# Cosine-weighted linear attention with an MoE tail: cos and sin parts stacked along the contraction

## The chip, the cores and the metric

One core of a Trainium2 chip. The metric is the device time of one execution in microseconds (us), median of several runs. The engines in the profile: PE is TensorE (matmul), PEld its weight loads, DVE VectorE, ACT ScalarE, POOL GpSimd, SP the engine that issues most loads.

## The reference

```python
q, k, v: [8, 8, 576, 64] float32          # batch, heads, positions, head size
cos_w, sin_w = cos(pi/2 * pos/576), sin(...)           # one pair per position
phi(x) = concatenate([relu(x) * cos_w, relu(x) * sin_w], axis=-1)      # 64 -> 128
kv  = einsum('bhsf,bhsd->bhfd', phi(k), v);   z = sum over s of phi(k)
num = einsum('bhsf,bhfd->bhsd', phi(q), kv);  den = phi(q) . z + 1e-6
x   = (num / den) as [4608, 512]
h   = x @ w_in [512, 2048];  g = h * sigmoid(beta * h);  out = g @ w_out [2048, 512]
```

Dividing num by den cancels any factor of a query row. So the kernels use 1 and tan for the query's two halves in place of cos and sin.

## The kernel before

The tokens go through the MoE in nine chunks of 512. Each chunk has 32 slots on TensorE: 16 h groups (x @ w_in, then Silu on ScalarE), then 16 quarters of the out product. The attention of batch c+1 is slipped between the slots of chunk c. Batch 0 runs alone in a prologue, batch 1 beside chunk 0. A batch has 8 heads in 4 pairs of rows (j), 9 blocks (n) of 64 positions, and two halves (g) of the partitions. Line numbers in the profile mean: L260 the kv matmuls, L281 num, L366 h, L391 out.

```python
# keys: relu only; values: scaled twice, by cos and by sin; column D of vb holds cos or sin
vb = [P, NQ, 4, 2, E]; rk = [P, NQ, 4, D]; qb = [P, 2, NQ, 2*D]; qt, qs = [P, 2, NQ, P]
...
def kv_mm(b, jp, bank, jjs=(0, 1)):                       # 36 matmuls of 64x64, 130 columns (72 a batch)
    for n in range(NQ):
        for jj in jjs:
            for g in range(2):
                matmul(t[jj*HP:(jj+1)*HP, g], lhsT=rk[hs, n, 2*jp+jj, :],
                       rhs=vb[hs, n, 2*jp+jj] as (s e), start=(n == 0), stop=(n == NQ-1))
def num_mm(n, jp, bank, slot):                            # 8 matmuls of 64x64, 65 columns
    for cs in range(2):
        for jj in range(2):
            for g in range(2):
                matmul(ps[cols, bank+jj, ...], lhsT=(qt, qs)[cs][rows, jp, n, cols],
                       rhs=kv[rows, g, jp, cs, :], start=(cs == 0), stop=(cs == 1))
...
# prologue: GpSimd's part is two products with the broadcast table
take("act", 0); take("dve", 1)
v_scale(0, 1, 0, 0, 6, eng="pool")        # one tensor_tensor, 6 x 2 x 64 = 768 elements
take("act", 1)
v_scale(0, 1, 0, 6, NQ, eng="act")
v_scale(0, 0, 0); k_relu(0, 0, 2, "act", 0, 5); k_relu(0, 0, 2, "dve", 5, NQ); take("dve", 0)
kv_mm(0, 0, 6)
v_scale(0, 1, 1, 0, 5, eng="pool")        # one tensor_tensor, 640 elements
...
# q's tan part is made after the transpose: GpSimd multiplies qt by a tan table into qs
```

## Time and profile before

| | before |
|---|---|
| time | 296.71 us, median of 3 runs (296.6 to 297.01) |
| span in the profile | 295.0 us |
| TensorE busy | 286.8 us (97%) |
| GpSimd busy | 73.8 us, of which 29.3 us are q's tan products |
| first h group starts | 18.06 us |
| a steady chunk | 30.3 us |

The prediction below shows the lines that its argument rests on. Each line has the start, the length, the engine, the line, the operation, its output and inputs, and how many instructions were merged.

```profile
9.06 1.47 POOL L205 TENSOR_TENSOR vb<-raw_v,sin 128x768 bf16<-128x768 f32 x1 [6.90 <-ACT qt L235]
...
12.20 1.26 POOL L205 TENSOR_TENSOR vb<-raw_v,sin 128x640 bf16<-128x640 f32 x1 [1.67 <-DMA raw_v<-in_v_dram]
...
18.06 0.59 PE L366 MATMUL ps<-xt,win 128*128 128x512 bf16 x2
```

GpSimd needs two instructions for its share of batch 0, 2.7 us in all. The prologue is over when the first h group starts at 18.06.

### The profile page before, as it was taken

To read this page: it belongs to the slowest core of one execution; us is meant where nothing else is said; L and a number is where in the kernel's file an instruction comes from. 1 tells how busy PE (TensorE), PEld (TensorE's weight loads), DVE (VectorE), ACT (ScalarE), POOL (GpSimd) and SP (SyncE) were. 2 spreads that over 40 slices of the span, in tenths; PEclk is the share of its full clock that TensorE was granted. 3 is DMA by queue.
4 is the path that set the end of the run, shared out by engine and by line. 5 is a ranking of instruction groups with operands and counts; after the bars stand their busy time and mean duration, and the time that the engine had idled before them with its cause. 6 is when DMAs were issued, how large, how long until landed. Compare 5 with 4: busy or idle time off the path is not lost.

```text
span 295.0 us, 7173 instructions
## 1 busy us (share of the span) xinstructions
PE 286.8 (97%) x3058; PEld 142.8 (48%) x3058; DVE 116.3 (39%) x296; ACT 140.1 (47%) x223; POOL 73.8 (25%) x88
## 2 busy tenths in 40 slices
PE   8799999999999999999999999999999999999994
PEld 7454455455445544454445544554455444444443
DVE  5989978662920293019500960077005000000000
ACT  5758826563247214731474137512760277137510
POOL 1350003252382026402550256015701210000000
PEclk9999999999999999999999999999999999999999
DMA  7999999597999089916992599139102810130033
GB/s 259 366 393 379 387 389 393 197 288 268 163 259 361 4 125 219 383 62 120 217 379 76 113 231 397 45 67 196 44 2 46 146 37 0 41 84 19 0 73 71
DMA packets 50256, 53.82 MB, mean 182 GB/s; under 512 B 30880, under 2 KB 31152, under 8 KB 50224
## 3 DMA queue, kind: packets, MB, share of 16 engines
q1 hardware_dynamic: 47504, 46.01, 51.6%
q0 software_dynamic: 2688, 7.34, 10.7%
q8 instruction: 24, 0.39, 0.6%
q14 instruction: 8, 0.07, 0.1%
q10 hardware_dynamic: 32, 0.01, 0.0%
HBM read 36.71 MB, written 9.44 MB: 156 GB/s over the span
## 4 chain that ended last, share of the span: by engine, by line
PE 85%; DVE 5%; DMA 5%; ACT 2%; issue 1%; DVEq 0%
PE ps L366 38%; PE ps L391 38%; DMA w_stage<-in_moe_w_out_dram 5%; DVE win L108 4%; PE ps L281 4%; PE ps L260 3%; PE ps L407 1%; PE ps L416 1%; ACT vb L213 1%; DVE qs L218 1%; DVE xs L303 0%; ACT g_t L373 0%; ACT rk L188 0%; PE ps L425 0%; PE ps L230 0%
## 5 line engine op out<-in xcount | busy, mean ns | idle before, releaser
L366 PE MATMUL ps<-xt,win 128*128 128x512 bf16 x576 | 128.1, 379 | 0.8 <-ACT g_t L373 0.5
L391 PE MATMUL ps<-wout,g_t 128*128 128x512 bf16 x560 | 124.5, 379 | 0.2 <-ACT wout L115 0.2
L373 ACT ACTIVATE g_t<-ps,beta 128x512 bf16<-128x512 f32 x144 | 98.4, 687 | 36.6 <-PE ps L366 36.6
L366 PEld LDWEIGHTS <-win 128*128 128x128 bf16 x576 | 55.3, 98 | 67.6 <-DVE win L108 1.4
L391 PEld LDWEIGHTS <-g_t 128*128 128x128 bf16 x560 | 53.9, 98 | 64.0 <-issue 0.4
L386 POOL DMA_DIRECT2D out_dram<-o_sb x56 | 36.5, 656 | 142.2 <-ACT o_sb L397 142.2
L397 ACT COPY o_sb<-ps 128x512 f32<-128x512 f32 x35 | 20.5, 586 | 98.2 <-PE ps L391 98.2
L218 POOL TENSOR_TENSOR qs<-qt,tanr 128x1152 bf16<-128x1152 bf16 x12 | 29.3, 2456 | 10.2 <-DMA qt<-qb 10.2
L272 DVE CAST kv<-ps 128x520 bf16<-128x520 f32 x6 | 4.2, 700 | 67.8 <-PE ps L260 67.8
L410 DVE COPY o_sb<-ps 128x256 f32<-128x256 f32 x1 | 0.4, 425 | 63.0 <-PE ps L407 63.0
L303 DVE TENSOR_TENSOR xs<-ps,rden 128x768 bf16<-128x768 f32 (+5 forms) x26 | 23.1, 890 | 0.8
L292 DVE TENSOR_TENSOR den<-ps,eps 128x12 f32<-128x12 f32 (+4 forms) x26 | 4.2, 161 | 33.5 <-PE ps L281 33.5
L215 DVE TENSOR_SCALAR vb<-raw_v,cos 128x256 bf16<-128x256 f32 x63 | 17.1, 347 | 0.0
L215 DVE TENSOR_SCALAR vb<-raw_v,sin 128x256 bf16<-128x256 f32 x54 | 14.7, 349 | 0.0
L281 PEld LDWEIGHTS <-qt 64*64 64x64 bf16 x576 | 10.6, 106 | 5.0 <-issue 4.3
L281 PE MATMUL ps<-kv,qt 64*64 64x65 bf16 x576 | 11.8, 195 | 0.4 <-ACT kv L270 0.2
L190 DVE TENSOR_SCALAR qb<-raw_q 128x1152 bf16<-128x1152 f32 x16 | 11.4, 752 | 1.3 <-DMA raw_q<-in_q_dram 1.3
L108 DVE CAST win<-w_stage 64x512 bf16<-64x512 f32 (+1 forms) x28 | 11.6, 414 | 0.6
L260 PE MATMUL ps<-vb,rk 64*64 64x130 bf16 x576 | 10.1, 218 | 1.6 <-ACT rk L188 1.6
L281 PE MATMUL ps<-kv,qs 64*64 64x65 bf16 x576 | 11.6, 193 | 0.0
L260 PEld LDWEIGHTS <-rk 64*64 64x64 bf16 x576 | 8.5, 106 | 5.7 <-issue 3.0
L281 PEld LDWEIGHTS <-qs 64*64 64x64 bf16 x576 | 10.4, 105 | 0.0
(56 smaller groups left out, 99.9 us busy)
## 6 DMA issues: line engine op xcount, KB each, us to landing
raw_v<-in_v_dram SPq DMA_DIRECT2D x7, 1152.0 KB, 10.2
raw_k<-in_k_dram SPq DMA_DIRECT2D x7, 1152.0 KB, 12.9
raw_q<-in_q_dram SPq DMA_DIRECT2D x7, 1152.0 KB, 7.4
out_dram<-o_sb POOLq DMA_DIRECT2D x56, 128.0 KB, 4.1
w_stage<-in_moe_w_out_dram SPq DMA_DIRECT2D x4, 1024.0 KB, 9.0
w_stage<-in_moe_w_in_dram SPq DMA_DIRECT2D x3, 1024.0 KB, 12.8
out_dram<-o_sb SPq DMA_DIRECT2D x14, 128.0 KB, 2.3
raw_q<-in_q_dram SPq DMA_DIRECT2D x2, 576.0 KB, 4.4
```

What stands on the lines that cost most here:

```text
L108: nc.vector.tensor_copy(o, a)
L190: nc.vector.tensor_scalar(dst, src, scalar1=0.0, scalar2=None, op0=ALU.max)
L215: nc.vector.tensor_scalar(o, a, scalar1=t[:, n : n + 1], scalar2=None, op0=ALU.mult)
L218: eng.tensor_tensor(dst.rearrange("q n (g p) -> q n g p", g=2), src.rearrange("q n (g p) -> q n g p", g=2), tanr[:, n0:n1].unsqueeze(2).to ...
L260: nc.tensor.matmul(t[jj * HP : (jj + 1) * HP, g], lhsT=rk[hs, n, 2 * jp + jj, :], rhs=vb[hs, n, 2 * jp + jj].rearrange("q s e -> q (s e)") ...
L281: nc.tensor.matmul(ps[cols, bank + jj, slot * E : (slot + 1) * E], lhsT=(qt, qs)[cs][rows, jp, n, cols], rhs=kv[rows, g, jp, cs, :], start ...
L303: nc.vector.tensor_tensor(o.rearrange("q j n s d -> q j (n s) d"), nv[:, :, a:z, :, 0:D].rearrange("q j n s d -> q j (n s) d"), rden[:, :, ...
L366: nc.tensor.matmul(ps[:, h_bank(c, jt)], lhsT=win[jt // 4][:, mi, (jt % 4) * P : (jt % 4 + 1) * P], rhs=xt[:, :, jp, g * HP : (g + 1) * HP ...
L373: nc.scalar.activation(g_t, ps[:, h_bank(c, jt)], AF.Silu, scale=beta[:, jt : jt + 1])
L386: eng.dma_start(out=out_v[bb, n][:, m0:m1], in_=o_sb[hf * HP : (hf + 1) * HP, m0:m1])
L391: nc.tensor.matmul(o_ps, lhsT=gs[c, jt][:, tt * P : (tt + 1) * P], rhs=wout[jt // 4][:, jt % 4, :], start=(jt == 0), stop=(jt == JT - 1))
L397: nc.scalar.copy(o_sb, o_ps)
```

## The change

The intent: stack the cos and the sin part of a head along the contraction. Keys are scaled (relu times cos, relu times sin) into one [positions, 128] operand, values are only cast, with a column of ones, and q gets its tan copy before the transpose. Then num needs no accumulation over cos and sin: one matmul with K=128 does both.

```diff
-    vb = one.tile([P, NQ, 4, 2, E], ...)     -    rk = one.tile([P, NQ, 4, D], ...)
+    vb = one.tile([P, NQ, 4, E], ...)        +    kb = one.tile([P, NQ, 4, 2, D], ...)
-    qt, qs [P, 2, NQ, P]                     +    qt [P, 2, NQ, 2, P]
...
+    def relu_scale(dst, src, kind, eng, n0, n1):
+        if eng == "dve":                      # fused, table broadcast from PSUM
+            for j in ...: nc.vector.scalar_tensor_tensor(dst[:, n0:n1, j], src, 0.0, t, op0=max, op1=mult)
+            return
+        for n in range(n0, n1):               # one instruction per block n
+            if eng == "act": nc.scalar.activation(dst[:, n], src[:, n], Relu, scale=t[:, n:n+1])
+            else: (nc.gpsimd if eng == "pool" else nc.vector).tensor_scalar(
+                      dst[:, n], src[:, n], scalar1=0.0, scalar2=t[:, n:n+1], op0=max, op1=mult)
...
     kv_mm:  lhsT=kb[hs, n, j] as (c d)  (64x128), rhs=vb[hs, n, j]  (65 columns)
     num_mm: 4 matmuls, lhsT=qt[:, jp, n, jj, cols]  (128x64), rhs=kv[:, g, 2*jp+jj, :]
...
 prologue:
-    v_scale(0, 1, 0, 0, 6, eng="pool")  ...  v_scale(0, 1, 1, 0, 5, eng="pool")
+    k_scale(0, 1, 0, "pool")            ...  k_scale(0, 1, 1, "pool", 0, 5)     # 9 and 5 pieces
 chunk 0:
+        1: lambda: q_turn_last(2, "dve"),     # transposes of block n=8, evicted on VectorE
-        25, 26: 18 transposes of batch 1      +   25, 26, 27: 36 transposes
 chunks 1 to 6:
-    (7, q_tan(b, 0)), (8, q_tan(b, 1)) on GpSimd
+    q_tan_all() on VectorE ahead of the DMA transpose of q, which doubles
```

(The order in which k and v are loaded is also swapped.)

More of the change, by code (lines that the diff above doesn't have):

```diff
@@ L120 @@
     GJ = [(0, 0), (0, 1), (1, 0), (1, 1)]
-    for name in "qvk":
+    for name in "qkv":
         for b in range(2):
@@ L128 @@
     nc.scalar.dma_start(out=beta16, in_=moe_beta.rearrange("(j p) -> j p", p=P))
+    load_raw(0, "k", 0, 2)
     load_raw(0, "v", 0, 2)
-    load_raw(0, "k", 0, 2)
-    load_raw(0, "v", 2, 4)
-    load_raw(0, "k", 2, 3)
-    load_raw(0, "k", 3, 4)
+    load_raw(0, "k", 2, 4)
+    load_raw(0, "v", 2, 3)
+    load_raw(0, "v", 3, 4)
     load_w("in", 0, 2)
@@ L151 @@
     eps9 = const.tile([P, NQ], FP32, name="eps9")
-    tanr = const.tile([P, NQ, HP], FP32, name="tanr")
     nc.scalar.activation(cos9, it9, AF.Sin, bias=halfpi, scale=-ANG)
@@ L161 @@
     make_identity(nc, ident)
-    vb = one.tile([P, NQ, 4, 2, E], BF16, name="vb")
-    rk = one.tile([P, NQ, 4, D], BF16, name="rk")
-    qb = one.tile([P, 2, NQ, 2 * D], BF16, name="qb")
-    qt = one.tile([P, 2, NQ, P], BF16, name="qt")
-    qs = one.tile([P, 2, NQ, P], BF16, name="qs")
-    kv = one.tile([P, 2, 2, 2, E], BF16, name="kv")
+    vb = one.tile([P, NQ, 4, E], BF16, name="vb")
+    kb = one.tile([P, NQ, 4, 2, D], BF16, name="kb")
+    qb = one.tile([P, 2, NQ, 2, 2, D], BF16, name="qb")
+    qt = one.tile([P, 2, NQ, 2, P], BF16, name="qt")
+    kv = one.tile([P, 2, 4, E], BF16, name="kv")
     xs = one.tile([P, NQ, 2, 2 * D], BF16, name="xs")
@@ L174 @@
     nc.vector.tensor_scalar(eps9, eps9, scalar1=EPS, scalar2=None, op0=ALU.mult)
-    for cs, t in ((0, cos9), (1, sin9)):
-        nc.vector.tensor_copy(vb[:, :, :, cs, D], t.unsqueeze(2).to_broadcast([P, NQ, 4]))
+    nc.vector.memset(vb[:, :, :, D], 1.0)
     xts = {}
@@ L190, in relu @@
             nc.vector.tensor_scalar(dst, src, scalar1=0.0, scalar2=None, op0=ALU.max)
-    def q_relu(b, jp, eng="dve"):
-        relu(qb[:, jp].rearrange("q n (j d) -> q j n d", j=2), raw_tile(b, "q")[:, 2 * jp : 2 * jp + 2], eng)
-    def k_relu(b, j0=0, j1=4, eng="dve", n0=0, n1=NQ):
-        relu(rk.rearrange("q n j d -> q j n d")[:, j0:j1, n0:n1], raw_tile(b, "k")[:, j0:j1, n0:n1], eng)
-    def v_scale(b, cs, jp=None, n0=0, n1=NQ, eng="dve"):
-        t = (cos9, sin9)[cs]
-        rv = raw_tile(b, "v")
-        js = slice(0, 4) if jp is None else slice(2 * jp, 2 * jp + 2)
-        if jp is not None and eng != "act":
-            if eng == "dve":
-                t = ps[:, 0, 16 * cs : 16 * cs + NQ]
-            (nc.gpsimd if eng == "pool" else nc.vector).tensor_tensor(
-                vb[:, n0:n1, js, cs, 0:D],
-                rv.rearrange("q j n d -> q n j d")[:, n0:n1, js],
-                t[:, n0:n1].unsqueeze(2).unsqueeze(3).to_broadcast([P, n1 - n0, 2, D]), op=ALU.mult)
+    SC = {"cos": (cos9, 0), "sin": (sin9, 16), "tan": (tan9, 32)}
@@ L209, in v_scale @@
+    def relu_scale(dst, src, kind, eng, n0, n1):
+        t, col = SC[kind]
+        if eng == "dve":
+            t = ps[:, 0, col : col + NQ]
+            for j in range(dst.shape[2]):
+                nc.vector.scalar_tensor_tensor(
+                    dst[:, n0:n1, j], src[:, n0:n1, j], 0.0,
+                    t[:, n0:n1].unsqueeze(2).to_broadcast([P, n1 - n0, D]), op0=ALU.max, op1=ALU.mult)
             return
         for n in range(n0, n1):
-            o, a = vb[:, n, js, cs, 0:D], rv[:, js, n, :]
@@ L212, in v_scale @@
             if eng == "act":
-                nc.scalar.activation(o, a, AF.Copy, scale=t[:, n : n + 1])
+                nc.scalar.activation(dst[:, n], src[:, n], AF.Relu, scale=t[:, n : n + 1])
             else:
-                nc.vector.tensor_scalar(o, a, scalar1=t[:, n : n + 1], scalar2=None, op0=ALU.mult)
-    def tan_mul(eng, dst, src, n0, n1):
-        eng.tensor_tensor(
-            dst.rearrange("q n (g p) -> q n g p", g=2), src.rearrange("q n (g p) -> q n g p", g=2),
-            tanr[:, n0:n1].unsqueeze(2).to_broadcast([P, n1 - n0, 2, HP]), op=ALU.mult)
@@ L222, in q_turn_pe @@
-    def q_turn_pe(b, jp, bank, hold=False):
-        parts = ((0, 0, 5), (1, 5, NQ))
-        v2 = []
-        for i, n0, n1 in parts:
-            t = ps[:, bank + i].bitcast(BF16)[:, 0 : (n1 - n0) * P].rearrange("q (n c) -> q n c", c=P)
-            v2.append(t)
-            for n in range(n0, n1):
-                nc.tensor.matmul(t[:, n - n0, :], lhsT=qb[:, jp, n, :], rhs=ident,
-                                 is_transpose=True, start=(n == n0), stop=(n == n1 - 1))
-        def take(e, i):
-            _, n0, n1 = parts[i]
-            if e == "act":
-                nc.scalar.copy(qt[:, jp, n0:n1], v2[i])
-            else:
-                tan_mul(nc.vector, qs[:, jp, n0:n1], v2[i], n0, n1)
-        if hold:
-            return take
-        for e, i in (("act", 0), ("dve", 1), ("act", 1), ("dve", 0)):
-            take(e, i)
@@ L244, in q_turn_dma @@
-    def q_turn_dma(b):
-        nc.sync.dma_start(out=qt.rearrange("q s n c -> q (s n) c"),
-                          in_=qb.rearrange("q s n c -> q (s n c)"), transpose=True)
-    def q_tan(b, jp):
-        tan_mul(nc.gpsimd, qs[:, jp], qt[:, jp], 0, NQ)
-    def kv_out(jp, bank):
-        return ps[:, bank : bank + 2, jp * 2 * E : (jp + 1) * 2 * E]
-    def kv_mm(b, jp, bank, jjs=(0, 1)):
-        t = kv_out(jp, bank)
-        for n in range(NQ):
-            for jj in jjs:
+                (nc.gpsimd if eng == "pool" else nc.vector).tensor_scalar(
+                    dst[:, n], src[:, n], scalar1=0.0, scalar2=t[:, n : n + 1], op0=ALU.max, op1=ALU.mult)
@@ new lines, in q_relu, with q_tan, q_tan_all @@
+    def q_relu(b, jp, eng="dve"):
+        relu(qb[:, jp, :, :, 0].rearrange("q n j d -> q j n d"), raw_tile(b, "q")[:, 2 * jp : 2 * jp + 2], eng)
+    def q_tan(b, jp, eng, n0=0, n1=NQ):
+        relu_scale(qb[:, jp, :, :, 1], raw_tile(b, "q")[:, 2 * jp : 2 * jp + 2].rearrange("q j n d -> q n j d"),
+                   "tan", eng, n0, n1)
+    def q_tan_all():
+        for n in range(NQ):
+            nc.vector.tensor_scalar(qb[:, :, n, :, 1], qb[:, :, n, :, 0], scalar1=tan9[:, n : n + 1],
+                                    scalar2=None, op0=ALU.mult)
@@ new lines, in k_scale, with v_cast, q_turn_pe @@
+    def k_scale(b, cs, jp=None, eng="each", n0=0, n1=NQ):
+        js = slice(0, 4) if jp is None else slice(2 * jp, 2 * jp + 2)
+        relu_scale(kb[:, :, js, cs], raw_tile(b, "k")[:, js].rearrange("q j n d -> q n j d"),
+                   ("cos", "sin")[cs], eng, n0, n1)
+    def v_cast(b, j0=0, j1=4, eng="dve"):
+        o, a = vb[:, :, j0:j1, 0:D].rearrange("q n j d -> q j n d"), raw_tile(b, "v")[:, j0:j1]
+        (nc.scalar.copy if eng == "act" else nc.vector.tensor_copy)(o, a)
+    def q_turn_pe(blocks, bank):
+        for i, (jp, n, jj) in enumerate(blocks):
+            nc.tensor.matmul(ps[:, bank + i // 8].bitcast(BF16)[:, (i % 8) * P : (i % 8 + 1) * P],
+                             lhsT=qb[:, jp, n, jj].rearrange("q c d -> q (c d)"), rhs=ident,
+                             is_transpose=True, start=(i % 8 == 0), stop=(i % 8 == 7 or i == len(blocks) - 1))
@@ new lines, in q_turn_half, with q_take, q_turn_last @@
+    def q_turn_half(jp):
+        return [(jp, n, jj) for n in range(8) for jj in range(2)]
+    def q_take(jp, hf, bank, eng):
+        o = qt[:, jp, 4 * hf : 4 * hf + 4].rearrange("q n j c -> q (n j c)")
+        (nc.scalar.copy if eng == "act" else nc.vector.tensor_copy)(o, ps[:, bank].bitcast(BF16)[:, 0 : 8 * P])
+    def q_turn_last(bank, eng):
+        q_turn_pe([(jp, 8, jj) for jp in range(2) for jj in range(2)], bank)
+        (nc.scalar.copy if eng == "act" else nc.vector.tensor_copy)(
+            qt[:, :, 8], ps[:, bank].bitcast(BF16)[:, 0 : 4 * P].rearrange("q (s j c) -> q s j c", s=2, j=2))
@@ L258, in kv_mm @@
+    def q_turn_dma(b):
+        nc.sync.dma_start(out=qt.rearrange("q s n j c -> q (s n j) c"),
+                          in_=qb.rearrange("q s n j c d -> q (s n j c d)"), transpose=True)
+    def kv_mm(b, jp, bank):
+        for j in range(2 * jp, 2 * jp + 2):
+            for n in range(NQ):
                 for g in range(2):
@@ L260, in kv_mm @@
                     nc.tensor.matmul(
-                        t[jj * HP : (jj + 1) * HP, g], lhsT=rk[hs, n, 2 * jp + jj, :],
-                        rhs=vb[hs, n, 2 * jp + jj].rearrange("q s e -> q (s e)"),
+                        ps[:, bank + g, j * E : (j + 1) * E],
+                        lhsT=kb[hs, n, j].rearrange("q c d -> q (c d)"), rhs=vb[hs, n, j],
                         start=(n == 0), stop=(n == NQ - 1))
     def kv_take(jps, bank, eng="dve"):
-        a0, a1 = jps[0], jps[-1] + 1
-        o = kv[:, :, a0:a1].rearrange("q g s c e -> q g (s c e)")
-        a = ps[:, bank : bank + 2, a0 * 2 * E : a1 * 2 * E]
-        if eng == "act":
-            nc.scalar.copy(o, a)
-        else:
-            nc.vector.tensor_copy(o, a)
-    def num_mm(n, jp, bank, slot):
-        for cs in range(2):
-            for jj in range(2):
-                rows = slice(jj * HP, (jj + 1) * HP)
-                for g in range(2):
-                    cols = slice(g * HP, (g + 1) * HP)
-                    nc.tensor.matmul(
-                        ps[cols, bank + jj, slot * E : (slot + 1) * E],
-                        lhsT=(qt, qs)[cs][rows, jp, n, cols],
-                        rhs=kv[rows, g, jp, cs, :],
-                        start=(cs == 0), stop=(cs == 1))
+        j0, j1 = 2 * jps[0], 2 * jps[-1] + 2
+        o = kv[:, :, j0:j1].rearrange("q g j e -> q g (j e)")
+        a = ps[:, bank : bank + 2, j0 * E : j1 * E]
+        (nc.scalar.copy if eng == "act" else nc.vector.tensor_copy)(o, a)
+    def num_mm(n, jp, bank, slot):
+        for jj in range(2):
+            for g in range(2):
+                cols = slice(g * HP, (g + 1) * HP)
+                nc.tensor.matmul(
+                    ps[cols, bank + jj, slot * E : (slot + 1) * E],
+                    lhsT=qt[:, jp, n, jj, cols], rhs=kv[:, g, 2 * jp + jj, :],
+                    start=True, stop=True)
     def x_rden(bank, slot, n0, n1, jps):
@@ L421 @@
     warm_pe(58, 48)
-    for bank, n0, n1 in ((6, 0, 5), (7, 5, NQ)):
-        for n in range(n0, n1):
-            nc.tensor.matmul(ps[:, bank, (n - n0) * HP : (n - n0 + 1) * HP],
-                             lhsT=tan9[0:HP, n : n + 1].to_broadcast([HP, P]), rhs=identf,
-                             is_transpose=True, start=(n == n0), stop=(n == n1 - 1))
     nc.tensor.transpose(ps[:, 1, 0:JT], beta16, identf[0:JT, 0:JT])
-    for bank, n0, n1 in ((6, 0, 5), (7, 5, NQ)):
-        nc.vector.tensor_copy(tanr[:, n0:n1, :].rearrange("q n p -> q (n p)"), ps[:, bank, 0 : (n1 - n0) * HP])
-    q_relu(0, 0)
+    for t, col in SC.values():
+        nc.vector.tensor_copy(ps[:, 0, col : col + NQ], t)
     nc.vector.tensor_copy(beta, ps[:, 1, 0:JT])
-    nc.vector.tensor_copy(ps[:, 0, 0:NQ], cos9)
-    nc.vector.tensor_copy(ps[:, 0, 16 : 16 + NQ], sin9)
-    q_relu(0, 1)
-    warm_pe(8, 128, bank=0 + 2)
-    q_turn_pe(0, 0, 4)
-    nc.vector.reciprocal(rbeta, beta)
-    warm_pe(4, 128)
-    take = q_turn_pe(0, 1, 2, hold=True)
-    warm_pe(7)
-    take("act", 0)
-    take("dve", 1)
-    v_scale(0, 1, 0, 0, 6, eng="pool")
-    take("act", 1)
-    v_scale(0, 1, 0, 6, NQ, eng="act")
-    v_scale(0, 0, 0)
-    k_relu(0, 0, 2, "act", 0, 5)
-    k_relu(0, 0, 2, "dve", 5, NQ)
-    take("dve", 0)
+    nc.vector.reciprocal(rbeta, beta)
+    q_relu(0, 0, "act")
+    q_tan(0, 0, "dve")
+    q_relu(0, 1, "act")
+    q_tan(0, 1, "dve")
+    warm_pe(24, 128, bank=2)
+    q_turn_pe(q_turn_half(0), 4)
+    q_take(0, 0, 4, "act")
+    q_take(0, 1, 5, "dve")
+    warm_pe(6, 128)
+    q_turn_pe(q_turn_half(1), 2)
+    warm_pe(6)
+    q_take(1, 0, 2, "act")
+    k_scale(0, 1, 0, "pool")
+    k_scale(0, 0, 0, "dve")
+    v_cast(0, 0, 1, "act")
+    v_cast(0, 1, 2, "dve")
+    q_take(1, 1, 3, "dve")
     kv_mm(0, 0, 6)
-    v_scale(0, 1, 1, 0, 5, eng="pool")
-    v_scale(0, 0, 1)
+    k_scale(0, 1, 1, "pool", 0, 5)
+    k_scale(0, 0, 1, "dve")
     kv_take((0,), 6, eng="act")
-    v_scale(0, 1, 1, 5, NQ, eng="act")
-    k_relu(0, 2, 3, "act")
-    k_relu(0, 3, 4, "act", 5, NQ)
+    k_scale(0, 1, 1, "act", 5, NQ)
+    v_cast(0, 2, 3, "act")
     for i in range(1, 4):
@@ L465 @@
     got2 = x_rden(4, 0, 7, 8, (0,))
-    k_relu(0, 3, 4, "dve", 0, 5)
+    v_cast(0, 3, 4, "dve")
     warm_pe(2, bank=1)
@@ L507, in rest @@
         load_w("out", 1)
+        load_raw(1, "k")
         load_raw(1, "v")
-        load_raw(1, "k")
         load_w("out", 2)
@@ L514, in rest @@
         cast_wout(1)
-        v_scale(1, 0)
-        k_relu(1)
+        k_scale(1, 0)
+        v_cast(1)
         cast_wout(2)
-        q_relu(1, 0)
     def num_seven(jp, bank):
@@ L523, in num_seven @@
             num_mm(n, jp, bank, n)
-    takes = []
-    turns = (("act", 0), ("dve", 1), ("act", 1), ("dve", 0))
     early = {
+        1: lambda: q_turn_last(2, "dve"),
         3: lambda: (num_mm(8, 0, 2, 0), num_mm(8, 1, 2, 1), rest()),
         7: lambda: x_turn_pe(0, 8, 9, 6),
-        15: lambda: v_scale(1, 1, eng="act"),
-        22: lambda: (kv_mm(1, 0, 6), kv_mm(1, 1, 6), kv_take((0, 1), 6, "act"), q_relu(1, 1)),
-        25: lambda: takes.append(q_turn_pe(1, 0, 4, hold=True)),
-        26: lambda: (takes.append(q_turn_pe(1, 1, 6, hold=True)),
-                     [takes[0](*t) for t in turns], cast_wout(3, "addd"),
-                     [takes[1](*t) for t in turns]),
+        15: lambda: k_scale(1, 1, eng="act"),
+        22: lambda: (kv_mm(1, 0, 6), kv_mm(1, 1, 6), kv_take((0, 1), 6, "act"),
+                     [(q_relu(1, jp), q_tan(1, jp, "act", 0, 5), q_tan(1, jp, "each", 5, NQ)) for jp in range(2)]),
+        25: lambda: q_turn_pe(q_turn_half(0), 4),
+        26: lambda: (q_turn_pe(q_turn_half(1), 6),
+                     q_take(0, 0, 4, "act"), q_take(0, 1, 5, "dve"), cast_wout(3, "addd"),
+                     q_take(1, 0, 6, "act"), q_take(1, 1, 7, "dve")),
+        27: lambda: q_turn_last(4, "act"),
         28: lambda: (num_seven(0, 4), x_mul(x_rden(4, 0, 0, 7, (0,)), 0, 7)),
@@ L552, in load_next @@
         def load_next():
-            for name in "qvk":
+            for name in "qkv":
                 if b + 1 < B:
@@ L558, in att_units @@
             (0, lambda: num_rest() if b == 2 else None),
-            (0, lambda: (q_relu(b, 0), q_relu(b, 1), q_turn_dma(b), load_next())),
-            (1, lambda: v_scale(b, 0)),
-            (4, lambda: k_relu(b)),
-            (6, lambda: v_scale(b, 1)),
-            (7, lambda: q_tan(b, 0)),
-            (8, lambda: q_tan(b, 1)),
+            (0, lambda: (q_relu(b, 0), q_relu(b, 1), q_tan_all(), q_turn_dma(b), load_next())),
+            (1, lambda: k_scale(b, 0)),
+            (4, lambda: v_cast(b)),
+            (6, lambda: k_scale(b, 1)),
             (12, lambda: (kv_mm(b, 0, 6), kv_mm(b, 1, 6), kv_take((0, 1), 6))),
@@ L580 @@
         if slot == 24:
-            for name in "qvk":
+            for name in "qkv":
                 load_raw(2, name)
```

## The prediction

> **What bounds the kernel now.** I read the page first: busy shares, the 40 slices, and the chain that ended last.
>
> ```profile
> PE 286.8 (97%) x3058; PEld 142.8 (48%) x3058; DVE 116.3 (39%) x296; ACT 140.1 (47%) x223; POOL 73.8 (25%) x88
> ...
> DVE  5989978662920293019500960077005000000000
> ...
> PE 85%; DVE 5%; DMA 5%; ACT 2%; issue 1%; DVEq 0%
> ```
>
> TensorE (PE) is busy 97% of the span and carries 85% of the chain. VectorE is idle on average, but full in slices 2 to 7 (7 to 52 us). So there are two stages with different limits, and the change has to be priced in each. The chain in order of time says where one stage ends:
>
> ```profile
> 31.51 13.70 DMA w_stage<-in_moe_w_out_dram
> 45.24 0.73 ACT wout L115
> 46.01 1.02 PE ps L391 x4
> ...
> 94.99 1.15 PE ps L260 x72
> 96.13 2.70 PE ps L366 x12
> 98.83 2.59 PE ps L391 x12
> 101.42 1.36 PE ps L281 x138
> 102.78 11.33 PE ps L391 x52
> 114.11 11.22 PE ps L366 x52
> ```
>
> From 56.6 us the chain is TensorE alone: a chunk lasts 30.3 us, of which kv (L260) takes 1.15 us and num (L281) 1.36 us; the rest is the two large products. Before that, TensorE, VectorE and loads take turns. Here the timeline matters more than the chain, first VectorE's, then TensorE's (start, length, engine, line, operation, count, and in brackets the idle time before it):
>
> ```profile
> 18.55 5.09 DVE L108 CAST win<-w_stage 64x256 bf16<-64x256 f32 x12
> 23.68 0.16 DVE L292 TENSOR_TENSOR den<-ps,eps 128x4 f32<-128x4 f32 x1
> ...
> 41.86 1.43 DVE L190 TENSOR_SCALAR qb<-raw_q 128x1152 bf16<-128x1152 f32 x2 [1.34 <-DMA raw_q<-in_q_dram]
> ```
>
> ```profile
> 22.26 3.63 PE L366 MATMUL ps<-xt,win 128*128 128x512 bf16 x16
> ...
> 46.01 1.02 PE L391 MATMUL ps<-wout,g_t 128*128 128x512 bf16 x4 [0.16 <-ACT wout L115]
> ```
>
> VectorE casts weights from 18.55 to 23.64 in one piece, while TensorE has done its four h groups and the num of block n=8 by 22.26: TensorE is 1.4 us ahead there, and nothing makes it wait. At 46.01 it waits 0.16 us for the last weights; between 22.3 and 46 it is full. What delays TensorE in this stretch delays the end; what hastens it before 46 meets the weights.
>
> **What the Trainium skill says.**
> 1. "TensorE: Matmul & The Clock Gate", section "Back-to-back issue gap": a warm matmul of N columns costs N/2.4 + 2.5 ns. The trace agrees at N=512 (11.33 us / 52 = 218 ns, with the joints). For N=65 that is 29.6 ns, for N=130 56.7 ns.
> 2. The same page, "LDWEIGHTS": the load's time follows the number of columns and not the contraction length. So loading 128x64 should cost what 64x64 did, while kv's weights grow from 64 to 128 columns.
> 3. "TensorEngine Tiling (Array Packing)", "Restrictions": column tiling turns the fast weight load off. kv loses its column tiling, num keeps it. This trace can't show it for those shapes; but the 58 warm-up matmuls, with a 128-column load each and only 48 columns to stream, took 2.50 us, 43 ns apiece, so a 128-column load is no slower than 43 ns.
> 4. "VectorE: DVE Perf Modes", "The perf-mode tier table": a 16-bit tensor_scalar in SBUF may run at 4x, an fp32 one at 2x. The trace has the fp32 kind, 9 of 256 elements in 2.45 us.
>
> **Part by part.**
>
> *num.* Eight 64x64 matmuls per block and head pair become four of 128x64. Half the instructions, but not half the array time: before, four quadrants run side by side, after, two column halves. Both are two array passes of 65 columns: 9 x 2 x 2 = 36 passes a batch. The trace's starts of one quad after another (101.50, 101.57, 101.63 for the qt halves of successive blocks, two quads each) give 31 ns a pass, against 29.6 ns by point 1. So at most 36 x 1.5 = 0.05 us are to be had, perhaps 0.1 us with the smaller issue load. *kv.* 18 passes of 130 columns (18 x 56.7 = 1.02 us) become 36 passes of 65 (36 x 29.6 = 1.07 us): +0.05 us if loads stay hidden. Sum over 8 batches: -0.4 us at best, about 0 as the centre. The title's "one K=128 pass" saves nothing on the array.
>
> *Steady chunks, other engines.* GpSimd loses 12 tan multiplications (29.3 us), VectorE gains nine small bf16 ones a batch (estimated: 272 ns spacing of the fp32 kind less half of its 133 ns streaming = 0.2 us each, 1.85 us). The q transposes by DMA double from 18 to 36 blocks; they land in a median 6.5 us now, so some 10 to 13. In chunks 2 onward VectorE starts at 106, the transposes go at 110.3, and num comes at 131.8: hidden. In chunk 1 it is tighter. VectorE goes from 55.87 to 63.28 and kv starts at 64.53, a slack of 1.25 us against the added 1.85: +0.6 us, once.
>
> *Prologue.* Gone: the tan table's transposes and copies (1.2 us on PE, 0.85 on DVE) before q's relu. Added: the q tan product on VectorE (estimated from the 1349 ns of the 1152-element product with PSUM: 2 x 0.75 us per pair). q's transposes (32 in place of 18, still at 0.11 us each this early) end near 10 us. Keys land at about 9.0 us, when values did (GpSimd started on them at 9.06). Then GpSimd must make the sin keys of pair 0 alone: nine pieces of 128 elements. From its casts (396 ns at 256, 608 at 512: 184 fixed, 0.83 a element) that is 0.29 us, with gaps 0.34 us: done at 12.1, where the same work, shared with ScalarE, let kv start at 11.40. kv's second head can only follow the ninth piece: kv ends at about 12.5, was 12.1. For pair 1 ScalarE has four scaled pieces (1.3 us) and then a 576-element cast (0.67 us) after the eviction at 12.9: 14.85, where kv started at 14.33. I put the prologue at +0.6 us, on the path.
>
> *Chunk 0, slots 1 to 3.* The transposes of block n=8 move here, into the bank of the second h group, with their eviction on VectorE. That eviction stands behind all of win[1]'s casts in VectorE's order: earliest 23.64, done at 24.1, and num of n=8 needs it. TensorE, which resumed the h groups at 22.26, now does so at about 24.35: +2.1 us. Some 0.3 us of this comes back, since slots 8 to 15 took 7.23 us for 32 matmuls (6.9 without gaps) while waiting for casts, and now come later than these. Net +1.8 us.
>
> *Chunk 0, slots 22 to 28.* q of batch 1 needs 36 transposes on TensorE in place of 18: 18 x 56 ns = +1.0 us. ScalarE takes five tan pieces per pair (0.33 us each), after kv's eviction: with the 2.4 us by now it ends at 45.2 and 46.9, and TensorE comes for them at 45.35 and 47.1, so no wait, just. The last weights (landed at 45.2) are cast behind the evictions at about 48.6, and TensorE needs them at 49.1. The n=8 eviction shares bank 4 with the num that follows and stands behind another 1 us eviction on ScalarE: perhaps 0.2 us of wait. Against that, the 0.16 us wait at 46.01 vanishes. The stretch: +1.0.
>
> Sum: +0.6 +1.8 +1.0 -0.2 (waits that the shift fills) +0.6 +0 = +3.8 us as worked, with some of the small waits likely to overlap: I take +3.3, so 300.0 us.
>
> **Rivals.**
> *A: the array gains.* If num were bound by issue of its 2 x 144 instructions, halving these could save up to 0.7 us a batch, 5 us in all, and the kernel would come out even or at 294. For it: fewer instructions, and the small matmuls are 0.2 us long each in the profile. Against it: 31 ns a pass is within 5% of streaming.
> *B: weight loads become the bound in kv or num.* Each pass of kv now needs two loads of 128 columns in 29.6 ns. If these take 43 ns a pass: 36 x 13 = +0.5 us a batch, 4 us in all; if num's two halves don't load side by side, another 0.6 us a batch. Then 304 to 308. For it: the 43 ns bound is all the trace gives. Against: that figure is from the cold start, and the row halves read different partitions.
> *C: the chunk 0 delays are filled.* Before 46 us, loads run at 380 to 390 GB/s, and the last weights land at 45.2 whatever TensorE does. Had TensorE been waiting for them, delays would be free; it waited 0.16 us only. Then 297.5 at the least that I believe.
> *D: the doubled DMA transpose comes late in chunk 1*, where it goes at about 62.6 and is needed at 74.5: a wait only if it takes over 12 us; then +1 to 3 us.
>
> **Range and chances.** The middle is 300.0. Low 297.4 (C, with a little of A), high 304.0 (part of B or D). The 2% lines are 290.8 and 302.6. Faster needs all of A and no delay in chunk 0: 0.02. Slower needs B, D or a longer prologue: 0.18. Within: 0.80.
>
> **What would show it.** Chunk length in the steady part: kv 1.15 and num 1.36 us of each 30.3 should both stay within 0.15 us; kv at 1.6 or more is B, num at 0.9 or less is A. VectorE's timeline: the eviction into qt at about 24 us, after the twelve casts, and TensorE's h groups resuming just behind it (2 us after slot 3) rather than at 22.3; if not, the largest term is wrong. GpSimd's nine key pieces from 9.0 to about 12.1. TensorE's wait at slot 28 for weights gone, first steady h group about 3 us later. A wait of num for qt's DMA in chunk 1 would be D.

## The result, and the profile after

The changed kernel took 303.25 us (median of 4 runs, 303.12 to 303.97) against 296.65 us for the kernel before in the same rounds (296.3 to 297.01): 6.6 us or 2.3% slower. The ratio is 1.0227, with a 95% interval of 1.0207 to 1.0248. Ratios here are the mean time of one kernel's fast runs over that of the other's in the same rounds, so not quite the ratio of the medians.

The page of the kernel after: busy shares, the slices of VectorE and GpSimd and of TensorE's granted clock (the share of its full clock that the profile shows as allowed), the chain by engine (the work that ended last, followed back), and GpSimd's group (count, busy us, mean ns of one).

```profile
PE 290.7 (96%) x2526; PEld 146.5 (49%) x2526; DVE 127.5 (42%) x357; ACT 143.7 (48%) x228; POOL 49.6 (16%) x88
...
DVE  5659997485591059105920592049204000000000
...
POOL 1890000500141014101410141013101210000000
PEclk9869999999999999999999999999999999999999
...
PE 89%; DVE 4%; DMA 2%; POOL 2%; ACT 1%; issue 0%; SPq 0%; DVEq 0%; POOLq 0%
...
L206 POOL TENSOR_SCALAR kb<-raw_k,sin 128x128 bf16<-128x128 f32 x14 | 9.7, 703 | 6.3 <-DMA raw_k<-in_k_dram 6.3
```

GpSimd does less in all (49.6 us, was 73.8), yet it has come onto the chain with 2% of the span. It is full in slices 1 and 2, where VectorE is now half idle. Fourteen pieces of 128 elements took 703 ns each. The chain in order of time says what they held up:

```profile
8.44 6.27 POOL kb L206 x9
14.70 0.05 issue
14.75 0.73 PE ps L261 x20
...
26.16 0.38 PE ps L233 x4
26.55 0.45 PE ps L361 x2
26.99 0.00 issue
27.00 0.42 DVE win L109
27.42 0.03 issue
27.45 0.44 DVE qt L248
...
69.05 2.37 DVE kb L206 x9
71.42 0.05 issue
71.46 1.02 PE ps L261 x56
...
101.61 1.20 PE ps L261 x72
...
108.10 1.29 PE ps L277 x72
109.38 11.33 PE ps L386 x52
120.71 11.22 PE ps L361 x52
```

(In this kernel L261 is kv, L277 num, L361 h, L386 out, L233 q's transposes.) Three delays stand in it one after another: GpSimd's nine pieces before the first kv; VectorE's casts and then the eviction of block n=8 before num at slot 3 of chunk 0; VectorE's last key pieces before kv of batch 2. In the steady part kv takes 1.20 us (1.15 before) and num 1.29 (1.36).

TensorE's timeline in the prologue shows how it waits, two matmuls for each of GpSimd's pieces:

```profile
10.50 0.30 PE L261 MATMUL ps<-vb,kb 64*128 64x65 bf16 x6
11.29 0.20 PE L261 MATMUL ps<-vb,kb 64*128 64x65 bf16 x2 [0.49 <-POOL kb L206]
11.98 0.20 PE L261 MATMUL ps<-vb,kb 64*128 64x65 bf16 x2 [0.49 <-POOL kb L206]
...
22.25 0.59 PE L361 MATMUL ps<-xt,win 128*128 128x512 bf16 x2
...
28.18 3.63 PE L361 MATMUL ps<-xt,win 128*128 128x512 bf16 x16
```

Taking the same work in both profiles, the delay builds up as follows:

| work | before | after | delay so far | added here |
|---|---|---|---|---|
| first h group of chunk 0 | 18.06 | 22.25 | 4.19 | +4.19 |
| h groups of slot 4 | 22.26 | 28.18 | 5.92 | +1.73 |
| out product, slot 16 | 33.06 | 38.67 | 5.61 | -0.31 |
| out product, slot 28 | 46.01 | 52.34 | 6.33 | +0.72 |
| chunk 1 starts | 51.60 | 57.92 | 6.32 | -0.01 |
| kv of batch 2 done | 65.68 | 72.49 | 6.81 | +0.49 |
| num of batch 2 done | 72.44 | 79.06 | 6.62 | -0.19 |
| last out product | 287.29 | 293.81 | 6.52 | -0.10 |

The last 215 us, with five batches of the new num and kv, give back 0.10 us. Nearly two thirds of the loss are made before TensorE's first h group.

There is a second effect in the prologue, the granted clock. Stretches of 4 us, with TensorE's granted clock behind the engines' busy times, the kernel after:

```profile
12.00:16.00 4.00, 2.08 (x31) 1.10 (x33) 1.42 (x2) 0.47 (x2) 4.00 (x6) 0.68 1.03 364
16.00:20.00 4.00, 4.00 (x86) 2.54 (x87) 2.24 (x6) 2.43 (x8) 3.88 (x7) 0.50 1.05 390
```

The fourth column from the right gives GpSimd (4.00 of 4.00 us), the third from the right the clock: 0.68, then 0.50. The kernel before has 1.00 in both stretches. The Trainium skill, "TensorE: Matmul & The Clock Gate", Part 1, says that the clock gate falls to half after an idle window of some 3.4 us. The trace agrees with the half, but TensorE was not idle that long: between 10.5 and 14.75 us it waited 0.49 us at a time, and in the 3.41 us before the clock fell, at about 13.45, the profile has it busy for 1.43 us. The clock stayed at 0.50 until about 20.25.

The low clock is part of the same 4.19 us. From 14.75 on, the chain has no wait for GpSimd; TensorE works there, slowly. The second kv took 1.22 us (36 matmuls, 0.72 in e7 below at a clock of 1.00) and the num of pair 1 took 0.96 us (0.70 in e1 below at 1.00). Together that is 0.76 us, an estimate of its share: a faster TensorE could have met GpSimd's last piece, done at 18.16. The six runs of e3 below fit it: the two with a mean clock of 0.985 and 0.986 took 300.2 us on average, the four at 0.999 to 1.0 took 299.3, though their loads may have differed too.

### The profile page after: what moved, and what is told of

The parts are those of the page before. It is cut to its first block, busy times and chain, and to the rows that moved or that the text cites. A ratio compares the mean times of both kernels' runs of the same rounds, so it can differ in the third digit from the quotient of the medians.

```text
span 301.5 us, 6165 instructions
## 1 busy us (share of the span) xinstructions
PE 290.7 (96%) x2526; PEld 146.5 (49%) x2526; DVE 127.5 (42%) x357; ACT 143.7 (48%) x228; POOL 49.6 (16%) x88
## 4 chain that ended last, share of the span: by engine, by line
PE 89%; DVE 4%; DMA 2%; POOL 2%; ACT 1%; issue 0%; SPq 0%; DVEq 0%; POOLq 0%
PE ps L386 40%; PE ps L361 38%; PE ps L277 4%; PE ps L261 3%; DMA raw_k<-in_k_dram 2%; POOL kb L206 2%; DVE kb L206 2%; PE ps L402 1%; PE ps L233 1%; PE ps L411 1%; ACT xt L340 1%; DVE qb L218 1%; DVE qb L188 0%; PE ps L335 0%; DVE vb L228 0%
## 5 line engine op out<-in xcount | busy, mean ns | idle before, releaser
L361 PE MATMUL ps<-xt,win 128*128 128x512 bf16 x576 | 127.9, 379 | 0.8 <-ACT g_t L368 0.5
L386 PE MATMUL ps<-wout,g_t 128*128 128x512 bf16 x560 | 124.5, 379 | 0.0
L361 PEld LDWEIGHTS <-win 128*128 128x128 bf16 x576 | 55.4, 98 | 66.6 <-issue 1.4
L386 PEld LDWEIGHTS <-g_t 128*128 128x128 bf16 x560 | 53.9, 98 | 63.4
L206 DVE TENSOR_SCALAR kb<-raw_k,cos 128x256 bf16<-128x256 f32 x63 | 17.1, 345 | 0.0
L261 PE MATMUL ps<-vb,kb 64*128 64x65 bf16 x576 | 12.5, 195 | 3.0 <-POOL kb L206 2.9
L206 DVE TENSOR_SCALAR kb<-raw_k,sin 128x256 bf16<-128x256 f32 x54 | 14.7, 343 | 0.0
L261 PEld LDWEIGHTS <-kb 64*128 64x128 bf16 x576 | 10.5, 96 | 8.2 <-POOL kb L206 4.4
L277 PEld LDWEIGHTS <-qt 128*64 128x64 bf16 x576 | 10.9, 115 | 5.7 <-issue 4.7
L277 PE MATMUL ps<-kv,qt 128*64 128x65 bf16 x576 | 12.3, 200 | 0.5 <-DVE qt L248 0.5
L411 PE MATMUL ps<-zeros 128*128 128x48 bf16 (+2 forms) x101 | 10.3, 269 | 1.0 <-DVE zero_b L147 1.0
L218 DVE TENSOR_SCALAR qb<-qb,tan 128x256 bf16<-128x256 bf16 x54 | 11.1, 287 | 0.2
L228 DVE CAST vb<-raw_v 128x2304 bf16<-128x2304 f32 (+1 forms) x9 | 11.0, 1218 | 0.0
L206 POOL TENSOR_SCALAR kb<-raw_k,sin 128x128 bf16<-128x128 f32 x14 | 9.7, 703 | 6.3 <-DMA raw_k<-in_k_dram 6.3
## 6 DMA issues: line engine op xcount, KB each, us to landing
raw_k<-in_k_dram SPq DMA_DIRECT2D x7, 1152.0 KB, 10.5
```

What stands on the lines that cost most here:

```text
L206: (nc.gpsimd if eng == "pool" else nc.vector).tensor_scalar(dst[:, n], src[:, n], scalar1=0.0, scalar2=t[:, n : n + 1], op0=ALU.max, op1=A ...
L218: nc.vector.tensor_scalar(qb[:, :, n, :, 1], qb[:, :, n, :, 0], scalar1=tan9[:, n : n + 1], scalar2=None, op0=ALU.mult)
L261: nc.tensor.matmul(ps[:, bank + g, j * E : (j + 1) * E], lhsT=kb[hs, n, j].rearrange("q c d -> q (c d)"), rhs=vb[hs, n, j], start=(n == 0) ...
L277: nc.tensor.matmul(ps[cols, bank + jj, slot * E : (slot + 1) * E], lhsT=qt[:, jp, n, jj, cols], rhs=kv[:, g, 2 * jp + jj, :], start=True, ...
L361: nc.tensor.matmul(ps[:, h_bank(c, jt)], lhsT=win[jt // 4][:, mi, (jt % 4) * P : (jt % 4 + 1) * P], rhs=xt[:, :, jp, g * HP : (g + 1) * HP ...
L386: nc.tensor.matmul(o_ps, lhsT=gs[c, jt][:, tt * P : (tt + 1) * P], rhs=wout[jt // 4][:, jt % 4, :], start=(jt == 0), stop=(jt == JT - 1))
```

## The experiments

Theory P: GpSimd's pieces set the prologue. Rival Q: stacking itself does (32 transposes in place of 18, the tan product, the later values). Theory L: the eviction of block n=8 behind the weight casts costs TensorE 1.7 us in chunk 0. Rival F: TensorE runs into the casts anyway, so it is given back. All ratios are against the kernel before, which took 296.70 us (11 runs) beside the first four experiments and 296.82 us (9 runs) beside the last four. Every kernel is correct unless told otherwise.

### e1: the sin keys of batch 0 on VectorE

```diff
-    k_scale(0, 1, 0, "pool")
     k_scale(0, 0, 0, "dve")
+    k_scale(0, 1, 0, "dve")
...
-    k_scale(0, 1, 1, "pool", 0, 5)
     k_scale(0, 0, 1, "dve")
+    k_scale(0, 1, 1, "dve", 0, 5)
```

> The changed kernel with the sin keys of batch 0 made on VectorE (the same fused relu-times-table instruction as the cos keys) in place of GpSimd's pieces. Theory P (GpSimd's 14 pieces of 0.7 us set the prologue): VectorE is done with pair 0 at about 12.1 and pair 1 at about 15.1, where the second kv started at 17.94; the first h group starts near 19.4 in place of 22.25 and the time falls by about 2.8 us, to 300.4. Rival Q (the longer q path, 32 transposes and the tan product, or the later landing of keys and values sets the prologue): less than 0.7 us falls, 302.6 or more.

300.25 us, ratio 1.0121 (1.0108 to 1.0134): about 3.1 us less than the changed kernel (0.0106 of 296.7). TensorE's timeline:

```profile
14.54 0.45 PE L261 MATMUL ps<-vb,kb 64*128 64x65 bf16 x18 [0.50 <-ACT vb L228]
...
19.12 0.59 PE L361 MATMUL ps<-xt,win 128*128 128x512 bf16 x2
```

The first h group moved from 22.25 to 19.12, and the second kv now waits for casts of the values instead. P holds: the q path, unchanged here, allows the earlier start. The granted clock stayed at 1.00 between 12 and 20 us, so the 3.1 us hold the pieces and the low clock that followed them together.

### e2: the block n=8 evicted in the prologue, on ScalarE

```diff
     q_take(1, 1, 3, "dve")
+    q_turn_last(4, "act")
     kv_mm(0, 0, 6)
...
-        1: lambda: q_turn_last(2, "dve"),
```

> The changed kernel with the four transposes of block n=8 and their eviction moved out of slot 1 of chunk 0 into the prologue, before the first kv, where TensorE and ScalarE stand idle; eviction on ScalarE. Theory L (the eviction behind the weight casts on VectorE, and the bank shared with an h group, cost about 1.7 us of TensorE at slots 1 to 3, and these reach the end): the waits of 0.92 and 0.52 us vanish and the time falls by 1.4 to 1.8 us, to about 301.6. Rival F (TensorE runs into the weight casts in slots 4 to 15 anyway, so that most of it is taken back): it falls by less than 0.7 us, to 302.6 or more.

302.63 us, ratio 1.0201 (1.0184 to 1.0217): 0.8 us less than the changed kernel, and the two intervals overlap. By time alone this is at rival F's edge. The trace tells more:

```profile
26.33 3.63 PE L361 MATMUL ps<-xt,win 128*128 128x512 bf16 x16
```

Slot 4's h groups start at 26.33, 1.85 us earlier than after the change (28.18); counted from the first h group (22.16 here, 22.25 there) it is 1.76 us. So the two waits are gone as L says. The span fell by 1.2 us only (301.5 to 300.3), since part is given back at slot 25. Here is the chain of this kernel there:

```profile
44.23 2.70 PE ps L386 x12
46.93 0.11 issue
47.04 0.71 PE ps L233 x8
47.75 0.01 issue
47.76 0.62 PE ps L233 x8
```

The sixteen transposes of q of batch 1 end at 48.38, 1.45 us after TensorE was free, where after the change they take 0.89. VectorE still had its data only at 46.13 (46.26 after the change): q of batch 1 had not landed. So neither account was right as told: L's gain is real, and what takes a part of it back is the load of q, not the casts.

### e3: e1 and e2 together

```diff
     (the edits of e1 and e2)
```

> Both edits at once. If P and L hold and add: 303.25 - 2.8 - 1.6 = 298.9, which leaves about 2.2 us to the kernel before (rest of the prologue, doubled transposes of batch 1, VectorE's longer way in chunk 1). If they share a cause or the loads take over: 300 or more.

299.63 us, ratio 1.0098 (1.0082 to 1.0115), profiled span 297.3. Beside e1 that is 0.7 us by the ratios and 1.1 us by the spans. In e3's trace the keys landed 0.6 us later than in e1's (VectorE started on them at 8.99, not 8.43), and slot 4's h groups started at 23.85, not 25.05. Counted from the first h group (19.68 and 19.12) that is 4.17 us in place of 5.93, so L's term is 1.8 us. The two terms add in the trace; the expected 298.9 was missed by 0.7.

### e4: what a GpSimd piece costs, by form and by place

```diff
+    # in slot 5 of chunk 0 and in slot 1 of the last chunk, on scratch data, four of each:
+    tensor_scalar(max 0, mult pointer) 128;  the same 256;  tensor_scalar(mult pointer) 128
+    tensor_scalar(max 0) 128;  tensor_copy 128;  tensor_tensor(mult, broadcast table) 128
```

> The changed kernel with a GpSimd test added in two places where GpSimd has nothing to do, on scratch data: four each of relu-times-pointer of 128 elements (the form of the change), the same of 256, times pointer alone, max with a constant alone, plain cast, and tensor times broadcast table of 128. Once in chunk 0 beside a busy VectorE, once in the last chunk with VectorE idle. If the 0.7 us is the form's own price, it stays 0.7 in both places, and cast or constant forms take near 0.3; if it is contention with VectorE, it drops to about 0.3 in the last chunk. Time of the kernel: within 1 us of the changed kernel, 302.3 to 304.3.

GpSimd's timeline of this kernel, once beside a busy VectorE, once with VectorE idle (each line is four instructions):

```profile
23.14 3.39 POOL L564 TENSOR_SCALAR scratch<-srcq,sin 128x128 bf16<-128x128 f32 x4
26.51 4.98 POOL L566 TENSOR_SCALAR scratch<-srcq,sin 128x256 bf16<-128x256 f32 x4
31.49 3.83 POOL L569 TENSOR_SCALAR scratch<-srcq,sin 128x128 bf16<-128x128 f32 x4
35.29 3.63 POOL L572 TENSOR_SCALAR scratch<-srcq 128x128 bf16<-128x128 f32 x4
38.88 1.75 POOL L574 CAST scratch<-srcq 128x128 bf16<-128x128 f32 x4
40.60 1.91 POOL L576 TENSOR_TENSOR scratch<-srcq,sin 128x128 bf16<-128x128 f32 x4
...
246.08 2.80 POOL L564 TENSOR_SCALAR scratch<-srcq,sin 128x128 bf16<-128x128 f32 x4
248.88 4.48 POOL L566 TENSOR_SCALAR scratch<-srcq,sin 128x256 bf16<-128x256 f32 x4
253.36 2.34 POOL L569 TENSOR_SCALAR scratch<-srcq,sin 128x128 bf16<-128x128 f32 x4
255.68 1.99 POOL L572 TENSOR_SCALAR scratch<-srcq 128x128 bf16<-128x128 f32 x4
257.63 0.99 POOL L574 CAST scratch<-srcq 128x128 bf16<-128x128 f32 x4
258.60 1.47 POOL L576 TENSOR_TENSOR scratch<-srcq,sin 128x128 bf16<-128x128 f32 x4
```

Read the last six first, a quarter of each length. With VectorE idle the form of the change costs 0.70 us, just as in the prologue. So it is its own price and not contention. From 128 to 256 elements it grows by 0.42 us, 3.3 ns an element. A cast of 128 costs 0.25 us, so the prediction's 0.29 us for a piece was a cast's price. One operation less helps little: 0.59 us with the pointer alone, 0.50 with the constant alone. A product of tensors costs 0.37 us. Beside a busy VectorE (weight casts, and for the last two forms the scaling of w_out and of keys) all forms are dearer (0.85, 0.96, 0.91, 0.44, 0.48 us for 128 elements), and VectorE pays too: its casts of 64x512 took 486 ns on average in that stretch, 421 without the test. The single run, of unknown state, took 305.4 us, more than was expected. Its trace shows where: TensorE waited 2.26 us for the eviction of block n=8 behind VectorE's casts, 0.52 in the changed kernel, and from slot 4 to slot 16 it took 11.71 us, 10.49 there.

### e5: the kernel before, with GpSimd's work in pieces, and nothing else of the change

```diff
...
+            elif eng == "pool":
+                nc.gpsimd.tensor_scalar(o, a, scalar1=-1e30, scalar2=t[:, n:n+1], op0=max, op1=mult)
...
-    v_scale(0, 1, 0, 0, 6, eng="pool")
+    v_scale(0, 1, 0, eng="pool")
     take("act", 1)
-    v_scale(0, 1, 0, 6, NQ, eng="act")
```

> The kernel before, with one thing of the change alone: GpSimd makes its sin-scaled part of batch 0 (there of the values) in 9 + 5 pieces of 128 elements with a per-partition scalar, in place of one product of 768 with ScalarE's help and one of 640. Nothing else of the change is in it. Theory P: 14 pieces of 0.7 us from about 9.0 us end at 18.8, the second kv (was 14.33) follows, and the time rises by 4 to 4.5 us, to about 301. Rival Q (stacking itself, i.e. transposes, tan product or array shape, makes the prologue late): under 1.5 us.

As in the change, ScalarE's three blocks go to GpSimd too. 302.84 us, ratio 1.0207 (1.019 to 1.0225): 6.0 us more than the kernel before, so well above what either expectation said, on P's side. GpSimd's timeline:

```profile
8.40 11.47 POOL L215 TENSOR_SCALAR vb<-raw_v,sin 128x128 bf16<-128x128 f32 x14 [6.23 <-ACT qt L237]
19.94 4.39 POOL L106 CAST win<-w_stage 64x512 bf16<-64x512 f32 x8
```

Here the pieces come every 0.82 us (0.72 long, with gaps of 0.09), not every 0.70; why the gaps are there in this kernel and not in the changed one stays open. They end at 19.88, not at 18.8 as expected: 1.1 us. The rest of the excess goes with the low clock: it was 0.50 from 16 to 20 us and 0.56 from 20 to 24, and there the num of pair 1 took 1.03 us (0.64 before) and the eight transposes behind it 1.04 (0.62), 0.8 us more. The first h group starts at 24.33, 6.27 us late, just after ScalarE's copy of x (done at 24.29). The chain names GpSimd's weight casts, which end at 24.34, but in the kernel before the first h group started at 18.06 while these casts ran to 19.33: by the program it needs only the first four, done here at 22.54. With not one stacked matmul in it, GpSimd's pieces alone cost nearly what the whole change lost, though not as the same sum, since here they come more slowly.

### e7: GpSimd keeps the sin keys, but as one product per pair

```diff
-    k_scale(0, 1, 0, "pool")
+    k_sin_pool(0)            # nc.gpsimd.tensor_tensor(kb sin part, raw k, broadcast sin, mult): 1152 elements
-    k_scale(0, 1, 1, "pool", 0, 5)
+    k_sin_pool(1, 0, 5)      # 640 elements
```

> The changed kernel with GpSimd still making the sin keys of batch 0, but as one product with the table for each pair (1152 and 640 elements), without the relu: the result is wrong on purpose. By the kernel before (768 in 1.47 us, 640 in 1.26) this takes about 2.1 and 1.26 us. If the form of the instruction is the cause, GpSimd is done at 10.6 and near 14.0, and the time falls by 2.5 to 3.3 us, to about 300.2; if GpSimd as an engine is too slow beside VectorE whatever the form, it falls by less than 1.5.

300.00 us, ratio 1.011 (1.0093 to 1.0126), 3.5 us less than the changed kernel; the result is wrong, as intended.

```profile
8.56 2.11 POOL L228 TENSOR_TENSOR kb<-raw_k,sin 128x1152 bf16<-128x1152 f32 x1 [6.40 <-DMA raw_k<-in_k_dram]
11.47 1.26 POOL L228 TENSOR_TENSOR kb<-raw_k,sin 128x640 bf16<-128x640 f32 x1 [0.79 <-DMA raw_k<-in_k_dram]
```

The same engine, the same elements: 2.11 us in place of 6.27, and the first h group starts at 19.26 in place of 22.25. The missing relu does not explain it: in e4 a piece with the scalar alone still takes 0.59 us of 0.70. It is the form, not the engine. The clock fell here too, to 0.50 from about 16.9 to 20.1 us, so the gain does not rest on the clock alone.

### e6: q of batch 2 prepared earlier on VectorE

```diff
         31: lambda: (
+                     q_relu(2, 0), q_relu(2, 1), q_tan_all(0, 3),
                      [h_mm(1, jt, (0, 1)) for jt in range(2)], ...
-            (0, lambda: (q_relu(b, 0), q_relu(b, 1), q_tan_all(), q_turn_dma(b), load_next())),
+            (0, lambda: (q_tan_all(3) if b == 2 else (q_relu(b, 0), q_relu(b, 1), q_tan_all()), ...
```

> The changed kernel with batch 2's relu of q and three of its nine tan products moved ahead, into a stretch at the end of chunk 0 where VectorE waits 2.28 us for TensorE; nothing else. If VectorE's longer way in chunk 1 (1.85 us of tan products) is what delays kv there by 0.5 us, kv follows at once and the time falls by 0.4 to 0.6, to about 302.7; if something else holds kv (the loads), it stays at 303.2.

303.23 us, ratio 1.0222 (1.0206 to 1.0238): by time, nothing. In the trace the wait is gone: VectorE's key pieces end at 69.7, and kv of batch 2 follows the h groups without a gap.

```profile
63.26 7.93 PE L361 MATMUL ps<-xt,win 128*128 128x512 bf16 x36 [0.49 <-ACT g_t L368]
71.12 1.26 PE L261 MATMUL ps<-vb,kb 64*128 64x65 bf16 x72
```

From the start of chunk 1 (58.27) to the end of kv (72.38) it took 14.11 us, against 14.57 in the changed kernel. But this run's keys landed later and its chunk 1 started 0.35 us later. So the term of 0.46 us is there in the trace; as a difference of times it could not be told from the spread of the runs.

### e8: all repairs in one correct kernel

```diff
     (e2, e6, and e7 with its relu:)
+    k_sin_relu(0)            # nc.vector.tensor_scalar(max 0) in place, after v_cast(0, 1, 2)
...
     k_scale(0, 0, 1, "dve")
+    k_sin_relu(1, 0, 5)
+    v_cast(0, 3, 4, "dve")   # moved ahead of the reciprocals
```

> All repairs in one correct kernel: GpSimd's sin keys as a product with the table and the relu after it on VectorE, the eviction of the n=8 block in the prologue on ScalarE, one value cast ahead of the reciprocals, and batch 2's q early. If the terms are rightly told, only the 18 extra transposes of batch 1 (about 0.7 us), and up to 0.5 us of prologue stay, and the steady part gives nothing back: 297 to 298 us. If stacking has a gain that these delays had hidden, it comes out below 296.

297.71 us, ratio 1.0033 (1.002 to 1.0047). That is 5.5 us faster than the changed kernel by the medians (5.8 by the ratios), and 1 us slower than the kernel before.

```profile
17.65 0.59 PE L371 MATMUL ps<-xt,win 128*128 128x512 bf16 x2
...
46.84 1.03 PE L396 MATMUL ps<-wout,g_t 128*128 128x512 bf16 x4
```

The first h group starts 0.41 us earlier than before the change (18.06), slot 28 starts 0.83 us later (46.01). In between lie the 18 extra transposes of batch 1 (1.00 us) and, as in e2, a wait for its q: the transposes start 0.16 us late and the first sixteen take 1.17 us, 0.89 in the changed kernel. No gain of the stacking shows once the delays are taken out.

## Why the prediction was wrong

It expected 300.0 us; 303.25 came, inside its range of 297.4 to 304.0, but with twice the predicted change. The sign and most terms were right, and one was mis-sized by a factor of seven.

- **The step that failed**: "From its casts (396 ns at 256, 608 at 512: 184 fixed, 0.83 a element) that is 0.29 us, with gaps 0.34 us: done at 12.1". A piece took 0.70 us and the nine were done at 14.70. The term "I put the prologue at +0.6 us" measured +4.19. The line that was read is true for casts; the instruction that the change adds is another one, and the profile before had no example of it on GpSimd. e1, e5 and e7 tie the term to this instruction from three sides, e4 gives its price. Some 0.8 us of the 4.19 (the estimate above) is the low clock that the waits brought with them, which the prediction did not have at all. The start was misread as well: GpSimd's 9.06 before the change is put down to ScalarE's copy and not to the load, and the nine pieces started at 8.44.
- **num and kv**: predicted -0.05 to -0.1 and +0.05 us a batch; the chain shows -0.07 (1.36 to 1.29) and +0.05 (1.15 to 1.20). "The title's 'one K=128 pass' saves nothing on the array" held, and the times fit the reason, 36 passes before and after. By the page the 29.6 ns a pass are the gap of an isolated matmul; the traces gave 31 (num before, from the starts) and 33 (kv after).
- **Chunk 0, slots 1 to 3**: predicted +2.1 and then -0.3 back; measured +1.73 and -0.31. e2 shows that it is this eviction (1.76 us from the first h group to slot 4).
- **Chunk 0, slots 22 to 28**: predicted +1.0 - 0.2, though the +1.0 had already taken off the wait at 46.01; measured +0.72. The transposes took 1.00 us more (2.01 against 1.01), kv 0.05, and a gap of 0.33 us before slot 28 vanished.
- **Chunk 1**: predicted +0.6; measured +0.49, and e6's trace without it.
- **Steady chunks, other engines**: GpSimd's 29.3 us were indeed worth nothing, and the doubled transpose stayed hidden. The nine tan products took 1.85 us, as estimated.
- **Rivals**: A (issue-bound num) and B (weight loads in the way) are out with kv at 1.20 and num at 1.29 us. C (delays filled) did not happen in the changed kernel; e2 met a relative of it, the load of q. D showed no wait in the chain of chunk 1. None of the rivals was the one that came. A longer prologue was named as a way to come out slower, but with no size and no cause; GpSimd's time was in the sum, not among the rivals.

With 4.19 - 0.6 = 3.6 us of prologue taken off, the measured 6.5 us of span are 2.9, against the 3.3 predicted and the 3.8 as worked.

What stays open: how much exactly of the 4.19 us is TensorE's lower clock (0.76 us is an estimate), and why e5's pieces have gaps.

## What to carry to other kernels

Before taking a duration for a new instruction from the trace, check that the row is the same instruction on the same engine: a cast is no model for a scalar operation on GpSimd. Merging contraction halves into one matmul saves nothing where tiles of the array already ran side by side; count array passes and not instructions. A slow piece of work on an engine that is idle on average can still set the end, if it stands alone at the start, where nothing else can run.

## What the Trainium skill lacked or had wrong

- "GPSIMD Engine Reference", section 4.1 "Engine selection", says one-input work runs roughly at line rate there. The cast fits that (0.83 ns an element, from 396 ns at 256 and 608 at 512). The tensor_scalar of relu and a per-partition scalar does not: 0.70 us for 128 elements and 1.12 us for 256, so 3.3 ns an element; a product of two tensors (0.37 us for 128, 2.11 us for 1152) was the cheaper form. No page names a price for it.
- The same page tells of contention with VectorE without a size: beside a busy VectorE, 128 elements took 0.44 us in place of 0.25 (cast) and 0.96 in place of 0.59 (one scalar operation), and VectorE's casts rose from 421 to 486 ns on average.
- "TensorEngine Tiling (Array Packing)" gives no rate for 64x128 row tiles with a short moving operand: 36 passes of 65 columns with two 128-column loads each took 1.20 us, 33 ns a pass, so the loads stayed hidden.
- "TensorE: Matmul & The Clock Gate", Part 1, speaks of an idle window. Here the clock also fell when TensorE was far from idle by the profile: busy 1.43 us of the 3.41 before the fall in the changed kernel, and 1.99 of 3.45 in e7; in e1 it stayed at 1.00 with 1.92 of 3.41. No threshold follows from these.
